# Another order for the first four chunks of a retention and FFN kernel, with block 0's squares on ScalarE

## The chip, the core and the metric

The kernel runs on one core of one Trainium2 chip. The metric is the time of one execution on the device in microseconds, as the median over several runs. Engines are named as the profile names them: PE is TensorE (PEld its weight loads), DVE is VectorE, ACT is ScalarE, POOL is GpSimd, SP is SyncE, which here only issues transfers.

## What is computed

Retention over 8 batches, 8 heads, 576 positions and a head size of 64, then a feed-forward layer over the 4608 tokens that come out of it:

```python
scores = scale * np.matmul(q, k.transpose(0, 1, 3, 2))
Dmat = np.where(rel >= 0, gamma[:, None, None] ** rel[None, :, :], 0.0)
attn = np.matmul(scores * Dmat, v)
x = attn.transpose(0, 2, 1, 3).reshape(4608, 512)
h = np.maximum(x @ w_in, 0.0)        # w_in: 512 x 2048
out = (h * h) @ w_out                # w_out: 2048 x 512
```

q, k and v are float32. The two weights are float64 and are brought to float32 inside the kernel.

## The kernel before, in words

**Tiling.** The tokens are cut into 36 chunks of 128 for the retention and into 9 blocks of 512 (four chunks each) for the feed-forward layer. The span has two parts: up to about 550 us the chunks are worked through and, between them, the first weight product of the blocks; after it comes the second product of all blocks. Both products use a scheme with seven multiplications in place of eight (`PRODUCTS`), except the first product of block 0, which is done plainly in 16 pieces (`first_in`, L698), one for each 128 columns of `w_in`.

**A chunk.** `load(i)` issues the transfers of q, k and v from SP (chunk 0's k and v from ACT). `scale_q` (L384) multiplies q by its decay, on POOL, for chunk 0 on DVE. `scale_v` (L488) does the same for v on POOL. `turn_in` (L435) transposes k and q on PE into PSUM, and `turn_out` (L444) copies the two halves back to SBUF, on ACT or DVE. For the first four chunks `scores_full` (L532) forms the 128 x 128 scores of each head, DVE masks them in two instructions (L536), `carry_full` (L551) adds what comes from earlier chunks, and `retain_full` forms the chunk's own part (L557) and the new state (L560). ACT then copies the result into `xT` (L572) and the state into `u_sb` (L494). Later chunks use `scores` (L470, masked at L481), `retain_a`, `retain_b` and `retain_c` (L514, L589, L595).

**A weight piece.** `fetch_raw` issues the transfer of a raw float64 piece of 512 KB (L205). `convert(n)` runs the next n of a piece's six parts: one and two on DVE (L219, L223), one called `beside` on ACT (L227, L228), then three more on DVE (L231, L234, L237). A `first_in(j)` needs piece j done to L237. It takes four matmuls, of 512 columns at most; with `halves` and `at` it does only a part of the block's 512 tokens: `(0,)` is the first 256, and `(0, C)` the first 128 of a half. ACT then writes the ReLU into `g_room` (L703), and the square, L706 on DVE, is put into a list, `queue`, from which `some(2)` takes up to two entries in each later `first_in`.

**Order.** The order of the work is written out by hand: each engine executes its instructions in the order in which the program issues them, and between engines semaphores wait. The first four chunks are a straight list of calls from `warm(5)` on; after it a loop goes over the chunks and calls `ffn`, which runs `convert(6)` and a `step()` (one `first_in`) once or twice per half chunk, until block 0 is done. `warm(n)` issues n matmuls on a constant tile whose result isn't used (L861). Transfers of SP are issued in program order; each waits for the one that is eight before it.

Of the kernel before, what the change touches and what calls it, by code (L numbers as in the profile page):

```python
# [15 lines left out]
C = 128  # L16
# [24 lines left out]
def kernel(  # L41
# [97 lines left out]
    def load(i, names="qkv"):  # L139
        if i == 0:  # L140
            nc.sync.dma_start(dv, decays)
        got = loaded.setdefault(i, [None] * 3)
        for name, pool, src in (("q", ld3, q), ("k", ld5, k), ("v", ld4, v)):
            if name not in names:
                continue
            t = got["qkv".index(name)] = pool.tile([128, H, D], F32, tag=name, name=f"{name}_ld")

            issue = nc.scalar if i == 0 and name != "q" else nc.sync
            b, c0 = divmod(i * C, S)
            runs = [(b, c0, slice(0, C))] if c0 + C <= S else [(b, c0, slice(0, CH)), (b + 1, 0, slice(CH, C))]  # L150
            for e in range(1 if name == "v" else 2):
                for b, c0, to in runs:
                    at = src[b, :, c0:c0 + to.stop - to.start, :].rearrange("h s d -> s h d")
                    if name == "v":
                        issue.dma_start(t[to], at)
                    else:
                        issue.dma_start(t[to, e * HP:(e + 1) * HP, :], at[:, e::2, :])
# [138 lines left out]
    def fetch_raw(count):  # L296

        for _ in range(count):
            if n_raw[0] < min(N_W1, n_made[0] + N_RAW):
                fetch_w(n_raw[0])  # L300
                n_raw[0] += 1
# [18 lines left out]
    def convert(count):  # L320
        for _ in range(count):
            f = next(w_in_steps, None)
            f and f()
# [7 lines left out]
    load(1, "qk")  # L331
    fetch_raw(1)
    load(1, "v")
    fetch_raw(1)
    load(2)
    fetch_raw(1)

    make_identity(nc, ident)

# [38 lines left out]
        clean.add((half, bank))  # L378
        return new

    def scale_q(i, engine):
        t = loaded[i][0]
        at = N_PAT + i % N_PAT
        engine.tensor_tensor(t, t, dv[:, :, at:at + 1].to_broadcast([C, H, D]), op=ALU.mult)  # L384

# [35 lines left out]
    def turn_in(i, js=(1, 0)):  # L423

        if "p" not in st[i]:
            if i < N_EARLY:
                p = [ps_e.tile([128, 512], F32, tag=f"e{h}", name="t_ps") for h in range(2)]
            else:
                t = ps_t[0].tile([128, 2, 512], F32, tag="t", name="t_ps")
                p = [t[:, h, :] for h in range(2)]  # L430
            st[i]["p"] = [x.rearrange("p (j d t) -> p j d t", j=2, d=HP) for x in p]
        for j in js:
            for hp in range(HP):
                for h in range(2):
                    nc.tensor.transpose(st[i]["p"][h][:, j, hp, :], loaded[i][j][rows(h), 2 * hp:2 * hp + 2, :],  # L435
                                        ident[rows(h), rows(h)])
# [48 lines left out]
    def scale_v(i):  # L485
        vs = st[i]["vs"] = loaded[i][2]
        at = i % N_PAT
        nc.gpsimd.tensor_tensor(vs, vs, dv[:, :, at:at + 1].to_broadcast([C, H, D]), op=ALU.mult)  # L488
# [37 lines left out]
    def scores_full(i):  # L526


        sc = st[i]["sc"] = [ps_f.tile([128, HP, C], F32, tag="f", name="sc_ps") for e in range(2)]
        for hp in range(HP):  # L530
            for e in range(2):
                nc.tensor.matmul(sc[e][:, hp, :], lhsT=st[i]["kT"][rows(e), hp, :], rhs=st[i]["qT"][rows(e), hp, :],  # L532
                                 start=True, stop=True, skip_group_check=True)
        r = st[i]["ret"] = ret_room[i % 2]
        for e in range(2):
            nc.vector.tensor_tensor(r[:, e, :, :], sc[e], msk_full.to_broadcast([C, HP, C]), op=ALU.mult)  # L536
        scale_v(i)

    def x_full(hp, e, b):
        return xp[0][rows(b), e, 0:256].rearrange("p (g t) -> p g t", g=2)[:, hp % 2, :]  # L540
# [1 line left out]
    def carry_full(i):  # L542

        xp[0] = ps_x.tile([128, 2, 256], F32, tag="x", name="x_ps", padded_shape=[128, 2, 512])
        clean.clear()
        if i == 0:
            u_ps[0] = ps_u.tile([128, HP, D], F32, tag="u", name="u_ps")
            return
        u = u_sb[2 * i % 3]
        for hp, e, b in HEADS[0:2] + HEADS[4:6] + HEADS[2:4] + HEADS[6:8]:  # L550
            nc.tensor.matmul(x_full(hp, e, b), lhsT=u[rows(e), hp, :], rhs=st[i]["qT"][rows(e), hp, :],  # L551
                             start=clears(b, e), stop=False, skip_group_check=True)

    def retain_full(i):

        for hp, e, b in (HEADS[j] for j in (0, 4, 2, 6, 1, 5, 3, 7)):
            nc.tensor.matmul(x_full(hp, e, b), lhsT=st[i]["vs"][:, head(hp, e), :], rhs=st[i]["ret"][:, e, hp, :],  # L557
                             start=clears(b, e), stop=False, skip_group_check=True)
        for hp, e, b in HEADS:
            nc.tensor.matmul(u_ps[0][rows(e), hp, :], lhsT=loaded[i][1][:, 2 * hp + e, :], rhs=st[i]["vs"][:, head(hp, e), :],  # L560
                             start=(i == 0 and hp == 0), stop=(hp == HP - 1), skip_group_check=True)
        x_out(i, lambda: grown(i, 1))
# [120 lines left out]
    def some(count=1):  # L683
        for f in queue[:count]:
            f and f()
        del queue[:count]

    def first_in(j, halves=(0, 1), at=(0, HT)):

        assert n_made[0] > j  # L690
        wi, m, e = pieces[j]
        mp, mm = divmod(m, 2)
        p = ps_f.tile([128, 2, HT], F32, tag="f", name="h_ps")
        w = w_in[mp][:, mm, 2 * e:2 * e + 2, :, :].rearrange("p s c f -> p (s c) f")
        lo, hi = halves[0], halves[-1] + 1
        p = p[:, lo:hi, at[0]:at[1]]
        for c in range(N_DM):
            nc.tensor.matmul(p, lhsT=w[:, c, :], rhs=xT[0][:, c, :].rearrange("p (h t) -> p h t", h=2)[:, lo:hi, at[0]:at[1]],  # L698
                             start=(c == 0), stop=(c == N_DM - 1))

        t = g_room[mp % 2][:, 2:5:2, mm, :] if e else g_room[mp % 2][:, 0:4:3, mm, :]
        t = t[:, lo:hi, at[0]:at[1]]
        nc.scalar.activation(t, p, AF.Relu)  # L703

        some(2)
        queue.append(lambda: nc.vector.tensor_tensor(t, t, t, op=ALU.mult))  # L706
        if mm and e and hi == 2 and at[1] == HT:
            queue.append(lambda: [nc.sync.dma_start(
                g_dram[0, a:b, :, 2 * mp:2 * mp + 2, :].rearrange("s p m t -> p s (m t)"),
                g_room[mp % 2][:, a:b, :, :].rearrange("p s m t -> p s (m t)")) for a, b in QUARTERS])  # L710
        if j >= N_W1 - 4:

            sums_w.setdefault(0, sum_w_in(0)).pop(0)()
            if n_next[0] > 1:
                if 1 not in sums_x:
                    sums_x[1] = sum_x(1)
                sums_x[1].pop(0)()
# [78 lines left out]

    def block_steps(n):
        if n == 0:
            seconds = [(0, first_in, j, (1,), (C, HT)) for j in range(N_HALF)]
            return seconds + [(0, first_in, j) for j in range(N_HALF, N_W1)]  # L800
        return [(n, ffn_in, n, mp, j) for mp in range(N_MP) for j in range(NP)]

# [55 lines left out]
    def warm(count):  # L858
        t = ps_f.tile([128, 512], F32, tag="f", name="idle_ps")
        for _ in range(count):  # L860
            nc.tensor.matmul(t[:, 0:256], lhsT=idle, rhs=idle[:, 0:1].to_broadcast([128, 256]), start=True, stop=True)  # L861
# [10 lines left out]
            load(i + 3, "v")  # L872

    warm(5)
    scale_q(0, nc.vector)
    turn_in(0, (1,))
    scale_q(1, nc.gpsimd)
    warm(1)
    turn_in(0, (0,))
    turn_out(0)  # L880
    load(3)
    fetch_raw(2)
    warm(1)
    scores_full(0)
    turn(1, (0, 0))
# [4 lines left out]
    scores_full(1)  # L890
    scale_q(2, nc.gpsimd)
    carry_full(1)
    convert(2)
    retain_full(1)
    load(4)
    fetch_raw(3)
    load(5)
    convert(3)
    first_in(0, (0,))
    convert(3)  # L900
    turn(2, (0, 0))
    scores_full(2)
    scale_q(3, nc.gpsimd)
    carry_full(2)
    first_in(1, (0,))
    convert(2)
    retain_full(2)
    load(6)
    turn(3)
    convert(1)  # L910
    scores_full(3)
    scale_q(4, nc.gpsimd)
    convert(3)
    carry_full(3)
    for j in range(N_HALF):
        first_in(j, (1,), (0, C))
    early.close()
    ps_t[0] = first.enter_context(tc.tile_pool(name="ps_t", bufs=1, space=PS))
    convert(2)
    retain_full(3)  # L920
    load(7)
    convert(1)
    step()
    step()
    convert(3)
# [2 lines left out]
    convert(3)  # L928
    scores(4)
    scale_q(5, nc.gpsimd)  # L930
    convert(3)
    step()
    convert(3)
    for i in range(N_EARLY + 1, N_CH + 1):
        if i > N_ONE:
            move(C, i)
# [289 lines left out]
```

## Time and profile before

| | |
|---|---|
| median of 3 runs | 957.81 us (957.13 to 959.32) |
| profiled execution, its time | 957.27 us |
| profiled execution, its span | 955.5 us |
| PE busy over the span | 939.5 us, 98% |
| DVE busy | 786.7 us, 82% |
| ACT busy | 335.7 us, 35% |
| POOL busy | 126.0 us, 13% |

The page cuts the span into 40 slices of 23.9 us. Its rows of busy tenths, the granted TensorE clock and the transfers are:

```profile
PE   8999999999999999999999999999999999999998
DVE  5789899888899898888856588788878788787876
ACT  3444485666765775766610000000000000000000
POOL 4312222212213212212100000000000000000000
PEclk9999999999999999999999999999999999999999
DMA  9996476775767765863369984535445453525251
```

A digit is the busy share of a slice in tenths. The first four to five slices hold all the work that this document is about: chunks 0 to 9 and the 16 pieces of block 0. The first slice is the one with the most idle PE; in it and the next two the 16 transfer engines are busy to nine tenths.

### The profile page before, as it was taken

What the parts mean: (1) busy time and instruction counts of PE and PEld (TensorE: products, weight loads), DVE (VectorE), ACT (ScalarE), POOL (GpSimd) and SP (SyncE); (2) the same over time, 40 slices, a digit from 0 to 9 for tenths busy, and PEclk for the clock granted to TensorE, in tenths of its full rate; (3) what the DMA queues carried; (4) which work ended last, traced back from release to release, by engine and by line L of the source; (5) the groups of instructions that cost most, each with busy time, mean ns of one, the idle gap of its engine ahead of it and who ended that gap; (6) DMA issues with size and microseconds to landing.
All of it is one profiled execution on the core that took longest, in us unless ns stands there. A gap on an engine that the chain in (4) does not pass through costs nothing. (4 is left out here: it accounts for less than half of the span.)

```text
span 955.5 us, 23378 instructions
## 1 busy us (share of the span) xinstructions
PE 939.5 (98%) x9750; PEld 844.1 (88%) x9750; DVE 786.7 (82%) x1435; ACT 335.7 (35%) x798; POOL 126.0 (13%) x115
## 2 busy tenths in 40 slices
PE   8999999999999999999999999999999999999998
PEld 6654788888888888888888899999999999999998
DVE  5789899888899898888856588788878788787876
ACT  3444485666765775766610000000000000000000
POOL 4312222212213212212100000000000000000000
PEclk9999999999999999999999999999999999999999
DMA  9996476775767765863369984535445453525251
GB/s 228 235 278 147 131 222 159 208 234 181 199 182 237 216 183 172 274 187 117 144 212 353 354 282 168 187 114 186 170 154 190 172 190 142 199 100 176 93 174 45
DMA packets 172778, 181.43 MB, mean 190 GB/s; under 512 B 118784, under 2 KB 133248, under 8 KB 166016
## 3 DMA queue, kind: packets, MB, share of 16 engines
q1 hardware_dynamic: 170576, 179.41, 60.2%
q8 instruction: 76, 1.25, 0.6%
q10 hardware_dynamic: 2096, 0.52, 0.3%
q14 instruction: 30, 0.25, 0.1%
HBM read 109.39 MB, written 70.52 MB: 188 GB/s over the span
## 5 line engine op out<-in xcount | busy, mean ns | idle before, releaser
L734 PE MATMUL h_b<-room,w 128*128 128x256 f32 x768 | 182.0, 380 | 2.3 <-DVE room L753 1.9
L420 ACT COPY qk<-flip 32x256 f32<-32x256 f32 x416 | 167.4, 402 | 6.6
L734 PEld LDWEIGHTS h_b<-room,w 128*128 128x128 f32 x768 | 145.4, 190 | 23.5 <-DVE room L753 3.2
L1075 PE MATMUL o_b<-w,room 128*128 128x128 f32 x1168 | 144.4, 275 | 0.2 <-DVE room L1027 0.2
L1075 PEld LDWEIGHTS o_b<-w,room 128*128 128x128 f32 x1168 | 137.2, 192 | 0.4 <-DVE room L1027 0.4
L734 PE MATMUL h_a<-room,w 128*128 128x256 f32 x512 | 124.0, 384 | 0.8 <-issue 0.7
L1075 PE MATMUL o_c<-w,room 128*128 128x128 f32 x1008 | 123.0, 275 | 0.0
L734 PE MATMUL h_c<-room,w 128*128 128x256 f32 x512 | 121.0, 379 | 0.0
L1075 PEld LDWEIGHTS o_c<-w,room 128*128 128x128 f32 x1008 | 117.7, 192 | 0.0
L1089 ACT COPY r<-o_a 128x128 f32<-128x128 f32 x53 | 14.1, 266 | 271.9 <-PE o_a L1075 236.2
L734 PEld LDWEIGHTS h_c<-room,w 128*128 128x128 f32 x512 | 97.3, 190 | 13.2
L734 PEld LDWEIGHTS h_a<-room,w 128*128 128x128 f32 x512 | 95.1, 190 | 14.8 <-issue 1.2
L1075 PE MATMUL o_a<-w,a 128*128 128x128 f32 x688 | 85.6, 275 | 0.0
L751 POOL TENSOR_TENSOR room<-room 128x512 f32<-128x512 f32 x32 | 35.1, 1096 | 360.1 <-ACT room L750 284.4
L1075 PEld LDWEIGHTS o_a<-w,a 128*128 128x128 f32 x688 | 81.2, 192 | 0.1
L741 DVE SCALAR_TENSOR_TENSOR room<-room 128x512 f32<-128x512 f32 x96 | 73.5, 765 | 3.3
L698 PE MATMUL h_ps<-room,w 128*128 128x512 f32 (+2 forms) x160 | 59.6, 518 | 4.0 <-DVE w L237 2.6
L488 POOL TENSOR_TENSOR v_ld<-v_ld,dv 128x512 f32<-128x512 f32 x36 | 51.4, 1429 | 8.9 <-DMA v_ld<-in_v_dram 6.0
L753 DVE TENSOR_TENSOR room<-h_b,room 128x512 f32<-128x512 f32 x32 | 22.0, 688 | 37.0 <-PE h_b L734 37.0
L698 PEld LDWEIGHTS h_ps<-room,w 128*128 128x128 f32 x160 | 26.8, 190 | 28.1 <-issue 20.7
L595 PEld LDWEIGHTS x_ps<-qk,v_ld 64*64 64x64 f32 x1024 | 38.4, 134 | 12.7 <-issue 10.9
L595 PE MATMUL x_ps<-qk,v_ld 64*64 64x64 f32 x1024 | 48.3, 222 | 0.0
(113 smaller groups left out, 1352.1 us busy)
## 6 DMA issues: line engine op xcount, KB each, us to landing
g_dram<-room SPq DMA_DIRECT2D x164, 256.0 KB, 3.9
a<-g_dram SPq DMA_DIRECT2D x30, 1024.0 KB, 5.9
room<-g_dram SPq DMA_DIRECT2D x15, 1024.0 KB, 6.1
w<-w_dram SPq DMA_DIRECT2D x7, 1792.0 KB, 10.7
out_dram<-room SPq DMA_DIRECT2D x17, 512.0 KB, 3.3
q_ld<-in_q_dram SPq DMA_DIRECT2D x64, 128.0 KB, 4.3
w<-in_moe_w_in_dram SPq DMA_DIRECT2D x16, 512.0 KB, 6.3
w<-in_moe_w_out_dram SPq DMA_DIRECT2D x16, 512.0 KB, 4.4
```

Source lines behind the costliest of these rows:

```text
L420: nc.scalar.copy(*moves.pop(0)[2:])
L488: nc.gpsimd.tensor_tensor(vs, vs, dv[:, :, at:at + 1].to_broadcast([C, H, D]), op=ALU.mult)
L595: return [lambda hp=hp, e=e, b=b: nc.tensor.matmul(x_at(hp, e, b, h), lhsT=s["vs"][rows(h), head(hp, e), :], rhs=s["ret"][rows(h), e, hp, ...
L698: nc.tensor.matmul(p, lhsT=w[:, c, :], rhs=xT[0][:, c, :].rearrange("p (h t) -> p h t", h=2)[:, lo:hi, at[0]:at[1]], start=(c == 0), stop= ...
L734: nc.tensor.matmul(p[:, mm, :], lhsT=w[:, c, :], rhs=xs[n][right][:, c, :], start=(j in OPENS and mm == 0 and c == 0), stop=(j in CLOSES a ...
L741: nc.vector.scalar_tensor_tensor(t, t, 0.0, t, op0=ALU.max, op1=ALU.mult)
L751: nc.gpsimd.tensor_tensor(g["A11"], g["A11"], g["A11"], op=ALU.mult)
L753: nc.vector.tensor_tensor(g["A22"], p, p15, op=ALU.add)
L1075: nc.tensor.matmul(p, lhsT=s["lefts"][left][:, m, :], rhs=w_out[j][:, m, WO_SLOT[right], :], start=(i in OPENS and m == 0), stop=(i in CLO ...
L1089: nc.scalar.copy(r[:, 0, 0:128], p)
```

## The change

It has five parts.

1. Loads: chunk 2's q and k are issued ahead of the second raw weight piece, and its v behind it. The third raw piece is no longer issued between chunk 2 and chunk 3, but behind chunk 3 (`fetch_raw(3)` in place of `fetch_raw(2)`).
2. Chunk 0: its q is scaled in two halves of four heads; its v is scaled on POOL ahead of chunk 1's q, where it stood behind it; one of the single `warm` matmuls is gone.
3. Chunks 1 to 3: `turn(2)` stands right behind `retain_full(1)`, and `turn(3)` between `carry_full(2)` and `retain_full(2)`, each earlier by one `first_in`. Pieces 0 and 1 run over the first half of the block in two parts of 128 tokens each, placed behind a turned chunk or in front of a retain, and over the second half in one part of 256, where the second half was in two parts.
4. Conversion: the parts are put elsewhere between the chunks, in groups of three, and the last two groups ahead of the loop hold six parts each, so that 36 parts (six pieces) are issued ahead of the loop in place of 33.
5. Squares: where a `first_in` covers both halves (pieces 2 to 15), the square is an ACT instruction (`Square`) and no longer one of DVE; `some(2)` now stands ahead of the piece's own ReLU.

```diff
     load(1, "v")
+    load(2, "qk")
     fetch_raw(1)
-    load(2)
-    fetch_raw(1)
+    load(2, "v")
...
-    def scale_q(i, engine):
-        t = loaded[i][0]
+    def scale_q(i, engine, parts=(slice(0, H),)):
         at = N_PAT + i % N_PAT
-        engine.tensor_tensor(t, t, dv[:, :, at:at + 1].to_broadcast([C, H, D]), op=ALU.mult)
+        for heads in parts:
+            t = loaded[i][0][:, heads, :]
+            engine.tensor_tensor(t, t, dv[:, heads, at:at + 1].to_broadcast(list(t.shape)), op=ALU.mult)
...
-        scale_v(i)
+        if i:
+            scale_v(i)
...
+        some(2)
         nc.scalar.activation(t, p, AF.Relu)
-
-        some(2)
-        queue.append(lambda: nc.vector.tensor_tensor(t, t, t, op=ALU.mult))
+        if hi - lo == 2:
+            queue.append(lambda: nc.scalar.activation(t, t, AF.Square))
+        else:
+            queue.append(lambda: nc.vector.tensor_tensor(t, t, t, op=ALU.mult))
...
-            seconds = [(0, first_in, j, (1,), (C, HT)) for j in range(N_HALF)]
+            seconds = [(0, first_in, j, (1,)) for j in range(N_HALF)]
...
-    scale_q(0, nc.vector)
+    scale_q(0, nc.vector, (slice(0, HP), slice(HP, H)))
     turn_in(0, (1,))
+    scale_v(0)
     scale_q(1, nc.gpsimd)
-    warm(1)
     turn_in(0, (0,))
     turn_out(0)
     load(3)
-    fetch_raw(2)
+    fetch_raw(3)
...
     carry_full(1)
+    retain_full(1)
     convert(2)
-    retain_full(1)
+    turn(2, (0, 0))
     load(4)
     fetch_raw(3)
     load(5)
+    first_in(0, (0,), (0, C))
     convert(3)
-    first_in(0, (0,))
-    convert(3)
-    turn(2, (0, 0))
+    first_in(0, (0,), (C, HT))
     scores_full(2)
     scale_q(3, nc.gpsimd)
     carry_full(2)
-    first_in(1, (0,))
-    convert(2)
+    turn(3)
     retain_full(2)
     load(6)
-    turn(3)
-    convert(1)
+    convert(3)
     scores_full(3)
     scale_q(4, nc.gpsimd)
-    convert(3)
     carry_full(3)
-    for j in range(N_HALF):
-        first_in(j, (1,), (0, C))
+    first_in(1, (0,), (0, C))
     early.close()
...
-    convert(2)
+    convert(3)
     retain_full(3)
+    first_in(1, (0,), (C, HT))
+    convert(3)
     load(7)
-    convert(1)
     step()
     step()
...
-    convert(3)
+    convert(6)
     step()
-    convert(3)
+    convert(6)
```

## The prediction

> **What bounds the kernel now.** I read the whole span first: PE is busy for 939.5 of 955.5 us, so there are 16 us of idle PE in all, and only what shortens them, or PE's own work, can shorten the time. The chain of waits, followed back from the end, runs over PE's second product and tells nothing of the start. So next come the stages that the change touches, as busy time of the engines in three stretches. The columns are the stretch, its length, busy PE, PEld, DVE, ACT and POOL (instructions in brackets), the granted clock, the share of transfers and GB/s.
>
> ```profile
> 0.00:35.00 35.00, 29.15 (x382) 24.12 (x382) 21.43 (x35) 14.70 (x29) 12.14 (x21) 1.00 1.00 232
> 35.00:70.00 35.00, 34.85 (x403) 17.90 (x400) 29.59 (x48) 17.06 (x32) 8.20 (x7) 1.00 0.95 259
> 70.00:104.00 34.00, 31.37 (x437) 16.45 (x436) 32.37 (x49) 13.51 (x27) 7.81 (x6) 1.00 0.52 126
> ```
>
> PE idles 5.85 us up to 35 us, none to speak of up to 70, and 2.63 us from 70 to 104, where DVE is busy for 95% and ACT for 40%. Two separate prizes, then. The lists of waits say what PE waited for (us in total, times, longest); the last line is of 70 to 100 us, the others of 0 to 35.
>
> ```profile
> PE sc_ps L532 <- DVE qk L444: 1.2, 2, 0.9
> PE sc_ps L532 <- ACT qk L444: 1.2, 1, 1.2
> PE idle_ps L861 <- DVE w L329: 1.1, 1, 1.1
> PE h_ps L698 <- ACT w L227: 1.0, 1, 1.0
> PE x_ps L557 <- POOL v_ld L488: 0.5, 1, 0.5
> PE t_ps L435 <- DVE q_ld L384: 0.4, 1, 0.4
> ...
> PE h_ps L698 <- DVE w L237: 2.6, 3, 1.2
> ```
>
> Up to 35 us PE mostly stands between a turn and its scores, while the turned chunk is copied; in block 0 it waits three times for a converted weight. After 104 us PE is the bound again, so a shift at 104 us reaches the end. The rows that the sums use, in order of time (start, duration):
>
> ```profile
> 14.76 1.06 POOL L384 TENSOR_TENSOR q_ld<-q_ld,dv 128x512 f32<-128x512 f32 x1 [1.48 <-DMA q_ld<-in_q_dram]
> 14.93 1.43 DVE L237 SCALAR_TENSOR_TENSOR w<-w,w 128x512 uint32<-128x512 uint32 x1
> 18.17 1.38 POOL L488 TENSOR_TENSOR v_ld<-v_ld,dv 128x512 f32<-128x512 f32 x1 [2.35 <-DMA v_ld<-in_v_dram]
> 20.28 1.16 PE L532 MATMUL sc_ps<-qk 64*128 64x128 f32 x16 [1.16 <-ACT qk L444]
> 21.03 1.06 POOL L384 TENSOR_TENSOR q_ld<-q_ld,dv 128x512 f32<-128x512 f32 x1 [1.48 <-DMA q_ld<-in_q_dram]
> 39.34 3.70 PE L698 MATMUL h_ps<-room,w 128*128 128x512 f32 x8
> 98.10 3.70 PE L698 MATMUL h_ps<-room,w 128*128 128x512 f32 x8 [1.17 <-DVE w L237]
> ```
>
> And the groups of 35 to 104 us (busy, mean ns | idle before, releaser):
>
> ```profile
> L706 DVE TENSOR_TENSOR room<-room 128x512 f32<-128x512 f32 x13 | 8.9, 683 | 0.0
> L228 ACT ACTIVATE w<-w,exp_bias 128x512 uint32<-128x512 uint32 x12 | 8.7, 721 | 25.0 <-DVE w L219 25.0
> L227 ACT ACTIVATE w<-w 128x512 f32<-128x512 uint32 x12 | 8.3, 688 | 0.0
> ```
>
> **Chunk 0.** q's scaling is one instruction of 0.69 us at 6.05; two halves of 0.42 (the 128x256 squares, 416 ns) let the first four transposes start before the second half is done, so q's turn ends some 0.3 us earlier. Against it, v0 lands at 7.64 (issued 1.84, 5.8 to landing) and holds POOL to 8.70; chunk 1's q, scaled 8.20 to 9.26 now, then runs to 9.76 and its turn ends near 10.25 (now 9.8). The product that waited for v0 until 10.33 now finds it, and starts behind that turn at 10.25. Net: 0.1 us gained, which I count as nothing; ends -0.4 and +0.5.
>
> The warm matmul that goes (0.70 us from 5.66) stood in idle time. [...] Here the gap becomes 0.4 to 0.8 us, and the profile grants 1.00 even with gaps of 1.2. By the row: 0. [...] I take 0.
>
> **Chunks 1 to 3.** Transfers run at 232 GB/s here, about 1.1 us for 256 KB and 2.1 for a raw piece. Chunk 2's q, now scaled at 14.76, leaves piece 1 behind itself and lands near 12.8; POOL is with v1 until 13.27, so it is scaled by 14.35 (now 15.82). v2 has the same bytes ahead of it as before: 18.17. Chunk 3's q loses piece 2 ahead of it: near 19 (now 21.03), but POOL holds v2 until 19.55, so it is ready at 20.6. PE then, with durations of its rows:
> - chunk 1 ends at 15.5 as now; turn(2) to 16.2; meanwhile piece 0 is done on DVE at 15.7, not 16.36, since its last step no longer meets POOL's scaling (1.43 us where the clear ones take 0.69);
> - two parts of piece 0, 1.02 each, to 18.25. ACT's two copies of the turned chunk (1.07) run beside them, which is the 1.2 us wait of today. Scores(2) start at 18.25 (now 20.28) and end at 19.4, carry(2) at 20.0;
> - turn(3): k, then q at 20.65, to 21.05: a wait of 0.6, which is new, with retain(2) behind it. The mask (19.5 to 20.8) is ready, so retain(2) takes 21.05 to 22.55, beside chunk 3's copies on ACT and DVE (to 21.8); scores(3) to 23.7 (now start 27.01);
> - piece 1 on DVE behind that copy: three steps, one against v3's scaling on POOL, done at 24.3, and the mask of chunk 3 behind them to 25.6. Carry(3) to 24.3, a part of piece 1 to 25.35, retain(3) to 26.85, the other part to 27.8;
> - the second halves of pieces 0 and 1, 1.96 each, to 31.7. ACT has `xT` of chunk 3 at 27.6, just in time. turn(4), whose q lands at 28.36 as now, to 32.4 (now 35.1); piece 2 to 36.0, scores(4) to 36.6.
>
> Then **a new wait**: piece 3 needs L237, and on DVE its last three steps stand behind chunk 4's copy, which waits for ACT's copy, which stands behind ACT's ReLU (31.7 to 32.1), L227 and L228 (to 33.4). DVE copies until 34.7, squares a half (0.4), and takes 2.1 more: 37.1. Piece 3 starts at 37.2, 0.6 late. Now it starts at 39.34. **Gain of the head: 2.1 us.** Its low end is 0, if chunk 3's q still comes at 21.03 (every step from turn(3) on is then some 2 us later); its high end 3.2, if the new waits vanish.
>
> **Squares and conversion from 37 us on.** DVE loses 14 squares, 0.60 us apart back to back, or 8.4 us; ACT gains 14. [...] The square stands ahead of the next ReLU and behind L227 and L228; its own ReLU ended a piece (3.4 us) ago, so it stalls nothing. The instruction list of the changed kernel has one activation table load, as now.
>
> Against PE: piece 11 is ready at 77.21 today; eight squares fewer (4.8) and 0.8 for the later piece 3 give 73.2, and PE wants it at 77.27 - 0.57 - 2.1 = 74.6. Piece 14: 86.1 against 88.4. Piece 15: at most 91.6 against 93.4. Slack everywhere, about one or two collisions with POOL (0.75 each), so **2.6 us gained** (ends 1.2 and 2.6). The half piece of extra lead in the conversion costs no instruction and adds to that slack. The last square falls where ACT idles 1.5 and 3.9 us (104 to 111): nothing.
>
> **Sum.** Head 2.1 + block 0 2.6 = 4.7 us. The profiled execution took 957.27, so 952.6; the median of the runs lies 0.54 above it, so 957.81 - 4.7 = **953.1 us**. Behind 104 us one PE wait of 1.5 (at 145, for DVE with POOL beside it) may come or go; I leave it and widen by it.
>
> **Rivals.**
> - *The transfers don't follow the new order* (15 in 100): the three streams share the same engines, v2 and chunk 3's q land as now, and the head gains 0. For: the share of transfers is 1.00 up to 35 us. Against: landings today follow bytes issued. 957.8 - 2.6 = 955.2.
> - *One wait replaces another in block 0* (10 in 100): L231 waits for L227/L228, which stand behind squares; PE still waits for L237. 957.8 - 2.1 = 955.7. [...]
> - *ACT paces block 0* (slower, 7 in 100): each square holds ACT, and behind it the ReLU that frees PSUM, then the conversion. [...]
> - *More than the sum* (6 in 100): the wait at 145 goes too: 951.6.
>
> The forecast itself has the rest, 62 in 100. Within 0.2% (1.9 us, about what this kernel's runs can tell from no change) fall the low ends of the first two rivals, 12 in 100 in all; slower is the third rival and 1 more. Faster 0.80, same 0.12, slower 0.08. The range goes from 950.8 (head 3.2, block 0 2.6, the wait at 145 partly) to 956.5 (head 0, block 0 1.3).
>
> **What would show it.** Scores(2) at 18.3, scores(3) at 22.6, piece 2 at 32.4 and piece 3 at 37.2; chunk 3's q scaled from 19.6; no PE wait for L237 from 70 to 104, DVE there near 80% busy and ACT near 60%. It is wrong if chunk 3's q comes at 21, if piece 3 starts near 39, or if PE waits for a weight with ACT's L228 late.

## The result, and the profile after

The changed kernel takes 953.00 us (median of 4 runs, 952.74 to 954.21) beside 958.57 us for the kernel before on the same chip (4 runs, 957.13 to 960.01). The ratio is 0.9944 with a 95% interval of 0.9926 to 0.9963, so some 5.4 us are gone. The forecast was 953.1.

The profiled execution of the changed kernel took 954.21 us (span 952.5) and is the slowest of its four, where the one before, 957.27, was among the fastest of its kernel. So the two profiles differ by only 3.0 us in the span. A second profile of the unchanged new kernel (after_again, below) has a span of 950.5, which is 5.0 less. The shift is therefore followed place by place, with both profiles.

First the busy time of the engines of the changed kernel in the same three stretches as before:

```profile
0.00:35.00 35.00, 31.93 (x386) 25.65 (x387) 19.63 (x37) 14.89 (x30) 12.13 (x21) 1.00 0.95 216
35.00:70.00 35.00, 34.40 (x419) 17.51 (x421) 30.57 (x48) 21.61 (x40) 9.12 (x7) 1.00 1.09 282
70.00:104.00 34.00, 34.00 (x449) 20.31 (x442) 27.59 (x41) 18.56 (x35) 8.11 (x6) 1.00 0.52 133
```

PE is busy for 2.8 us more of the first 35 us, and from 70 to 104 it doesn't idle at all. DVE there fell from 95% to 27.59 / 34 = 81%, and ACT rose from 40% to 55%. The list of what PE waited for (us in total, times, longest) has five lines from 0 to 35 us; the last two are of 35 to 70, and from 70 to 104 there is none:

```profile
PE idle_ps L865 <- DVE w L329: 1.1, 1, 1.1
PE x_ps L553 <- ACT u_sb L495: 0.6, 1, 0.6
PE h_ps L700 <- DVE w L237: 0.4, 1, 0.4
PE sc_ps L533 <- DVE qk L445: 0.3, 1, 0.3
PE t_ps L436 <- DVE q_ld L385: 0.2, 1, 0.2
...
PE h_ps L700 <- DVE w L237: 0.3, 1, 0.3
PE sc_ps L471 <- DVE qk L445: 0.3, 1, 0.3
```

The three waits of scores for a turned chunk's copies up to 35 us (2.4 us in all before) are down to one of 0.3, and the wait of the first piece for ACT (1.0) and the three of 70 to 104 us (2.6) are gone. The rows of the changed kernel in order of time (start, duration), for the instructions that the prediction dated. The view of piece 3 ends at 40 us, so it counts seven of its eight matmuls:

```profile
18.37 1.16 PE L533 MATMUL sc_ps<-qk 64*128 64x128 f32 x16
19.65 1.06 POOL L385 TENSOR_TENSOR q_ld<-q_ld,dv 128x512 f32<-128x512 f32 x1
22.64 1.16 PE L533 MATMUL sc_ps<-qk 64*128 64x128 f32 x16
24.83 1.16 PE L700 MATMUL h_ps<-room,w 128*128 128x128 f32 x8 [0.42 <-DVE w L237]
32.59 3.70 PE L700 MATMUL h_ps<-room,w 128*128 128x512 f32 x8
37.23 3.27 PE L700 MATMUL h_ps<-room,w 128*128 128x512 f32 x7 [0.32 <-DVE w L237]
98.70 1.99 PE L738 MATMUL h_a<-room,w 128*128 128x256 f32 x8
```

The kernel before begins block 1 here:

```profile
103.75 1.99 PE L734 MATMUL h_a<-room,w 128*128 128x256 f32 x8
```

Scores(2) start at 18.37 where they started at 20.28, scores(3) at 22.64 (27.01), piece 3 at 37.23 (39.34), and block 1 at 98.70 (103.75). And the groups of the changed kernel from 35 to 104 us (busy, mean ns | idle before, releaser):

```profile
L708 ACT ACTIVATE room<-room 128x512 f32<-128x512 f32 x14 | 8.7, 620 | 0.0
L228 ACT ACTIVATE w<-w,exp_bias 128x512 uint32<-128x512 uint32 x12 | 8.7, 721 | 8.4 <-DVE w L219 8.3
```

L708 is the new square: 0.620 us each, and it never waited. ACT's idle time for DVE ahead of L228 fell from 25.0 to 8.3 us: its slack was spent and not exceeded.

**Where the gain goes afterwards.** The same product of PE, found in two traces, tells how far one runs ahead of the other. Below is the lead over the trace before, in us:

| place (time before) | after | second profile of after |
|---|---|---|
| block 1 begins (103.75) | 5.05 | 5.32 |
| about 153 | 5.04 | 5.34 |
| about 327 | 6.00 | 6.26 |
| about 370 | 2.37 | 4.36 |
| end of the first product (537) | 2.67 | 4.65 |
| end of the span | 3.01 | 5.00 |

The lead at 104 us is a little over the forecast 4.7 in these two traces; in a third with the same instructions up to there (e7_w_out_later, below) it is 3.40. Between 327 and 370 us some of it is lost, 3.6 us in one trace and 1.9 in the other. What PE waited for from 104 to 560 us in the changed kernel:

```profile
PE h_b L738 <- DVE room L757: 1.9, 2, 1.5
PE h_a L738 <- issue: 1.7, 1, 1.7
PE sc_ps L471 <- ACT qk L421: 0.5, 1, 0.5
PE h_b L738 <- DVE room L750: 0.3, 1, 0.3
```

The second line is new in its size. "issue" means that the engine stood still without waiting for anything that the profile shows. It is this row of the timeline:

```profile
333.62 0.69 PE L738 MATMUL h_a<-room,w 128*128 128x256 f32 x1 [1.67 <-issue]
```

Right behind it the granted clock (the number behind the last bracket) is at half for one stretch, and full again in the next:

```profile
333.70:337.20 3.50, 3.50 (x9) 2.79 (x10) 3.50 (x7) 0.30 (x1) 0.00 (x0) 0.51 0.64 168
337.20:340.70 3.50, 3.50 (x18) 3.09 (x17) 1.04 (x3) 3.37 (x9) 0.00 (x0) 1.00 0.94 258
```

PE gets through nine matmuls where the next stretch has eighteen. The half clock lasts 3.41 us, so by this trace it costs about 1.7 us on top of the stop of 1.67; together they are nearly all of the 3.6.

### The profile page after: what moved, and what is told of

The parts are those of the page before. It is cut to its first block, busy times and chain, and to the rows that moved or that the text cites. A ratio compares the mean times of both kernels' runs of the same rounds, so it can differ in the third digit from the quotient of the medians.

```text
span 952.5 us, 23368 instructions
## 1 busy us (share of the span) xinstructions
PE 940.9 (99%) x9748; PEld 845.9 (89%) x9748; DVE 777.9 (82%) x1422; ACT 344.0 (36%) x812; POOL 126.9 (13%) x115
## 5 line engine op out<-in xcount | busy, mean ns | idle before, releaser
L757 DVE TENSOR_TENSOR room<-h_b,room 128x512 f32<-128x512 f32 x32 | 22.0, 689 | 37.6 <-PE h_b L738 37.6
```

The costliest lines, as they stand in the source:

```text
L757: nc.vector.tensor_tensor(g["A22"], p, p15, op=ALU.add)
```

## The experiments

Four questions: is the head's gain one of the transfers or of the order of the products; do the squares or the larger lead of the conversion free PE in block 0; what does chunk 0's part do; and where do the 1.9 to 3.6 us go behind 327 us. Each kernel is timed beside the kernel before on the same chip, and the ratio compares those two. The chips differ a little: the kernel before had medians of 958.78 beside e1 to e4, 959.23 beside e5 to e7 and after_again, and 958.13 beside e8 to e11. "Piece 3" and "block 1" are their starts in the kernel's profile; e5 and e6 were timed once only.

| kernel | median us (runs) | ratio (95%) | piece 3 | block 1 |
|---|---|---|---|---|
| before | 958.57 (4) | | 39.34 | 103.75 |
| after | 953.00 (4) | 0.9944 (0.9926 to 0.9963) | 37.23 | 98.70 |
| e1_dve_squares | 954.73 (10) | 0.9968 (0.9956 to 0.9981) | 37.33 | 100.61 |
| e2_act_squares_alone | 954.51 (8) | 0.9961 (0.9947 to 0.9975) | 39.01 | 100.59 |
| e3_old_loads | 955.02 (8) | 0.9970 (0.9957 to 0.9982) | 39.22 | 101.33 |
| e4_new_loads_alone | 958.71 (8) | 1.0007 (0.9994 to 1.0021) | 39.68 | 105.99 |
| e5_old_chunk0 | 951.84 (1) | | 37.87 | 99.33 |
| e6_less_lead | 952.32 (1) | | 37.58 | 98.53 |
| after_again | 952.66 (2) | 0.9929 (0.9909 to 0.9949) | 36.86 | 98.43 |
| e7_w_out_later | 950.67 (4) | 0.9907 (0.9891 to 0.9924) | 37.93 | 100.35 |
| e8_lead_alone | 955.77 (6) | 0.9972 (0.9960 to 0.9984) | 39.76 | 103.33 |
| e9_dve_squares_less_lead | 956.11 (5) | 0.9997 (0.9961 to 1.0033) | 37.16 | 100.55 |
| e10_one_more_warm | 951.83 (4) | 0.9929 (0.9912 to 0.9945) | 37.55 | 99.58 |
| e11_warm_w_out | 951.22 (4) | 0.9925 (0.9910 to 0.9940) | 36.94 | 98.98 |

One thing to keep in mind for every row: three of these traces (after, after_again, e7_w_out_later) execute the very same instructions up to block 1, and their piece 3 starts at 37.23, 36.86 and 37.93, their block 1 between 98.43 and 100.35. A difference of under 1 us between two single traces of the head, or of under 2 at block 1, is weak evidence by itself; where two times bear on the same question, both are given. Taken together, the traces are firmer. The nine kernels or repeats with the new loads and the new order start piece 3 at 36.86 to 37.93 (middle value 37.33), the five that lack one or both at 39.01 to 39.76 (39.34). From piece 3 to block 1, the nine with the squares on ACT need 60.95 to 62.42 us (61.58), the five with them on DVE 63.28 to 66.31 (63.57). In neither case do the two groups overlap, and each step is worth 2.0 us by the middle values.

### The head: order of loads, order of products

The changed kernel with the loads in the old order:

```diff
-    load(2, "qk")
     fetch_raw(1)
-    load(2, "v")
+    load(2)
+    fetch_raw(1)
...
-    fetch_raw(3)
+    fetch_raw(2)
```

> The changed kernel with the loads in the order of before. Theory (the turned chunks can only move up because their q lands earlier): chunk 3's q is scaled at 21.0, turn(3) ends near 22.5, piece 3 starts at 38.5 to 39.3, so the head loses 1.3 to 2 of its 2.1 us; block 1 near 100.5. Rival (the order of the products does it, loads are early enough anyway): piece 3 within 0.4 us of 37.2.

Piece 3 started at 39.22: the new order of the products without the new loads gains nothing up to there. PE's list of waits from 0 to 36 us has a line that the first profiles of the two kernels lack (after_again has it with 0.3), and the timeline shows chunk 3's q scaled 1.9 us later than in the changed kernel:

```profile
PE t_ps L436 <- DMA k_ld<-in_k_dram: 1.2, 3, 0.8
```

```profile
21.57 1.06 POOL L385 TENSOR_TENSOR q_ld<-q_ld,dv 128x512 f32<-128x512 f32 x1 [1.72 <-PE sc_ps L533]
```

The row names PE's scores as what released POOL, but the second half of this q landed at 21.41, just before it (in the changed kernel at 19.49), so the transfer alone would have held it nearly as long. PE now waits for the transfer of a chunk's k, and turns chunk 2 at 17.20 (15.74 in the changed kernel) and chunk 3 at 22.1 (20.2). The kernel before with the new loads alone, the same edit the other way round:

> The kernel before with the new order of loads and nothing else changed. Theory: PE's order holds the turns behind the first pieces, so little is gained; piece 3 at 38.7 to 39.5, block 1 at 103.0 to 104.0. Rival (transfers alone are the bound of the head): piece 3 at 37.2 to 38.

The head gains nothing (39.68, just outside the expected 38.7 to 39.5), and the time is that of the kernel before. Block 1 at 105.99 was not expected; the trace puts it on one line (36 to 104 us):

```profile
PE h_ps L698 <- DVE w L237: 4.6, 4, 2.0
```

Five steps of DVE between 41 and 52 us fell on POOL's scalings and took 1.27 to 1.55 us each where the clear ones take 0.42 to 0.69. The median of its eight runs (958.71) shows no loss against the kernel before (958.78). This profile (959.21) is near that median, while the one of the kernel before that it is set against (957.27) lies below the median of its own; whether the collisions are of this execution alone was not tried. What follows: each half alone brings nothing up to piece 3, and the two together bring 2.1 us. The first turns need both the early q and k and an early place in the order. (That order was changed together with the splitting of pieces 0 and 1 and the places of the conversion parts; these were not tried apart.)

### Block 0: squares or lead

The changed kernel with the squares back on DVE:

```diff
         t = t[:, lo:hi, at[0]:at[1]]
-        some(2)
         nc.scalar.activation(t, p, AF.Relu)
-        if hi - lo == 2:
-            queue.append(lambda: nc.scalar.activation(t, t, AF.Square))
-        else:
-            queue.append(lambda: nc.vector.tensor_tensor(t, t, t, op=ALU.mult))
+
+        some(2)
+        queue.append(lambda: nc.vector.tensor_tensor(t, t, t, op=ALU.mult))
```

> The changed kernel with all squares of block 0 back on DVE; everything else is kept. Theory (head and block 0 are two separate gains): piece 3 starts at 37.2 as in the changed kernel, 2.1 earlier than before; PE waits again for L237 from 65 to 104 us, 2 to 3 us in all; block 1's first matmul starts near 101.7 (changed kernel 98.7, before 103.75), so some 2 us faster than before. Rival (the half piece of lead in the conversion did it, not the move to ACT): block 1 starts at 98.7 to 99.5 and the waits for L237 stay away.

And the kernel before with this edit of the change alone, the same lines the other way round:

> The kernel before with block 0's squares on ACT and nothing else changed. Theory: head as before (piece 3 at 39.3), no PE wait for L237 from 70 to 104, block 1 at 103.75 - 2.6 to 2.9 = 100.9 to 101.2. Rival (a wait for ACT takes the place of the wait for DVE without the extra lead): PE still waits 1 us or more for a weight, block 1 after 102.3.

The second did what it should. Its busy times from 35 to 104 us show DVE at 79% and 83% and a PE without a gap from 70 on:

```profile
35.00:70.00 35.00, 34.51 (x397) 17.71 (x397) 27.74 (x45) 20.42 (x38) 9.17 (x7) 1.00 0.98 267
70.00:104.00 34.00, 34.00 (x452) 19.28 (x451) 28.25 (x42) 18.73 (x36) 7.53 (x6) 1.00 0.52 131
```

From piece 3 to block 1 it needs 2.83 us less than the kernel before, and its time is lower by 0.39% (3.7 us). The first (e1_dve_squares) bears out neither theory: block 1 at 100.61 lies between the two forecasts, and the waits for L237 that were to come back did not. The same view of it shows:

```profile
35.00:70.00 35.00, 33.61 (x395) 17.30 (x394) 33.10 (x54) 18.24 (x32) 6.93 (x6) 1.00 1.00 268
70.00:104.00 34.00, 33.48 (x450) 19.19 (x449) 32.71 (x46) 14.05 (x27) 10.19 (x8) 1.00 0.55 141
```

DVE is busy for 95% and 96%, so it is full. PE's waits from 36 to 104 us are here 0.9 for the transfer of a k, 0.5 for DVE's copy of a turned chunk and 0.3 for L237. A theory from that: the larger lead of the conversion only moves the wait to other work of DVE. The next two kernels test it: the kernel before with three more parts converted ahead of the loop, and the changed kernel with the squares on DVE and three parts fewer.

```diff
     convert(3)
     step()
-    convert(3)
+    convert(6)
```

> The kernel before with half a piece more of conversion ahead of the loop (36 parts in place of 33) and nothing else changed; squares on DVE. Theory (either the lead or the move of the squares is enough to end the waits for L237 at the end of block 0, since the conversion comes to lead by a half piece or falls back by eight squares): the 2.6 us of such waits from 70 to 104 us shrink to under 1 us, block 1 starts at 101 to 102.5. Rival (only the move of the squares ends them, and the run with the squares back on DVE lacked them because other waits had put PE late): 2 us or more of waits stay, block 1 at 103 or later.

```diff
-    convert(6)
+    convert(3)
     step()
     convert(6)
```

(The second diff stands on top of that of e1_dve_squares.)

> The changed kernel with the squares on DVE and without the extra half piece of lead, so with neither of the two things that could end the waits for L237. Theory: 2 us or more of waits for L237 from 50 to 104 us come back, block 1 starts at 101.3 to 102.5. Rival (neither matters once the head is in its new order): no such waits, block 1 as with the lead, 100.6 or earlier.

PE's waits from 36 to 104 us, first with the lead alone, then with neither squares on ACT nor lead:

```profile
PE x_ps L595 <- DVE qk L481: 1.2, 1, 1.2
PE sc_ps L470 <- DVE qk L444: 0.7, 1, 0.7
```

```profile
PE h_ps L700 <- DVE w L237: 2.1, 4, 1.2
```

With the lead, PE waits for DVE's mask (L481) and DVE's copy of a turned chunk; without it, for the weight. The sum is about the same, 1.9 and 2.1 us. That much fits, and so does block 1 of the second: 100.55, as early as with the lead (100.61 in e1_dve_squares), where its theory had it at 101.3 or later. The times don't settle it: block 1 of the first starts at 103.33, only 0.4 us before that of the kernel before, while its six runs are 0.28% faster (2.7 us), of which the profiled one is the slowest (956.67); and the second's runs scatter from 953.35 to 964.8, so its time says nothing. How much the lead is worth on a DVE that is full stays open. Last, the changed kernel with squares on ACT but without that lead:

```diff
-    convert(6)
+    convert(3)
     step()
     convert(6)
```

> The changed kernel with three conversion parts ahead of the loop's last step in place of six, so that the conversion leads by half a piece less, as before. Theory: DVE has slack once the squares are gone; block 1 within 0.3 us of 98.7. Rival (the lead is what removes the waits for L237): 1 us or more of such waits come back, block 1 at 99.7 or later.

Block 1 at 98.53 against 98.70 and 98.43: as soon as DVE has room, the lead is not needed. So the squares carry block 0's gain: 2.83 us on the kernel before, and inside the changed one some 1.9 us (100.61 against 98.70), which is within the scatter of single traces. The groups of nine and five traces above back it, and so do the times: the ratio of e1_dve_squares, 0.9968, lies above both of the changed kernel, 0.9944 and 0.9929, though its interval overlaps the first one's.

### Chunk 0

The changed kernel with chunk 0 as it was:

```diff
-        if i:
-            scale_v(i)
+        scale_v(i)
...
-    scale_q(0, nc.vector, (slice(0, HP), slice(HP, H)))
+    scale_q(0, nc.vector)
     turn_in(0, (1,))
-    scale_v(0)
     scale_q(1, nc.gpsimd)
+    warm(1)
```

> The changed kernel with chunk 0 as before: q scaled in one instruction, v behind chunk 1's q on POOL, the warm matmul back. Theory: the split of q gains what v's new place on POOL costs, so chunk 1's scores and all that follows start within 0.2 us of the changed kernel; piece 3 at 37.0 to 37.4, granted clock 1.00 in both. Rival (the chunk 0 edits carry part of the head's gain): piece 3 0.4 us or more later.

Piece 3 came at 37.87, 0.64 later than in the first profile of the changed kernel, as the rival had it, but within the scatter of that same program (36.86 to 37.93). The part is worth less than can be seen in one trace: this does not contradict the forecast's "nothing", and a few tenths either way cannot be told.

### What is lost behind 327 us

A second profile of the unchanged new kernel:

> The changed kernel once more, unchanged, for its trace. In its profiled execution PE stood 1.7 us with no recorded reason at 332 us, and the granted clock was half for the 3.4 us after that, together 3.6 us. Theory (a chance event of that execution): block 1 starts at 98.7 again, the stop is elsewhere or absent, and the span is 949 to 951.5. Rival (the changed kernel causes it): again a stop of over 1 us near 332 us with half clock behind it, span 952.5.

The half clock did not come again, but the stop did: 1.63 us at 333.3. So the stop is no chance event of one execution. The half clock behind it comes and goes: of six traces with this stop, two have it (after and e1_dve_squares). Runs without a profile have their mean granted clock on record too, and one such stretch lowers it to 0.998. It is 0.998 or less in 9 of 30 runs of the kernels whose trace has the long stop, and in 4 of 85 runs of the others. In e1, e3 and e4 these runs are 1.7 to 2.3 us slower in the mean than the rest of their kernel's. So the half clock is rare without the stop and not certain with it.

Across all traces there is a pattern. PE stops at the same instruction of its list (4045 recorded matmuls stand ahead of it), for 1.4 to 1.7 us, in six of the seven traces of kernels that have one warm matmul fewer than before (after, after_again, e1, e3, e6, e9; e7 has only a stop of 0.3 near 405). It does so in none of the seven traces of kernels with as many PE instructions as before (before, e2, e4, e5, e8, e10, e11). Six of those seven stop elsewhere, near 220, for 0.45 to 0.69. The seventh, e11, stops near 404 for 0.53. A theory from that: the place where the stop falls, and its length, hang on how many instructions PE's list has ahead of it. It was tested by giving back one warm matmul, where PE is idle:

```diff
-    warm(5)
+    warm(6)
```

> The changed kernel with warm(6) in place of warm(5): PE has as many instructions ahead of everything later as before the change, whose warm matmul stood elsewhere. Five of six traces of kernels without that matmul show PE stopping for 1.6 to 1.7 us at the same instruction of its list (start 331 to 336 us), none of the four traces with it does; those stop 0.65 us at another one near 220 us. Theory (the stop belongs to the place in PE's instruction stream, with what the transfers do just then): no stop over 1 us near 332, 0.6 us near 218, the span about 1 us shorter than the changed kernel's, 949.5. Rival (the stop is caused by something else in the changed kernel): it stays at 1.6 us.

Of PE's waits from 104 to 560 us in this kernel, the one without a recorded reason is now:

```profile
PE h_a L738 <- issue: 0.4, 1, 0.4
```

The stop of 1.7 is gone, and one of 0.4 stands at 218 us, where the kernel before has its 0.69. Its lead over the trace before goes from 4.17 at block 1 to 5.13 at the end, where that of the second profile of after goes from 5.32 to 5.00. (Each lead begins with what its own head scattered by.) That is 0.96 gained against 0.32 lost, so the missing matmul costs 1.3 us in these traces. e5_old_chunk0, which has the matmul back in its old place, agrees: 4.42 to 5.40, and a stop of 0.65 at 218. The times do not show it: the ratio, 0.9929, is that of after_again. The theory holds in part. The count of PE's instructions moves the stop, but it does not decide alone: e7_w_out_later has the very PE list of the changed kernel and stops only for 0.3 near 405.

What goes with the stop shows in the transfers of after between 329 and 334 us (packets, MB, share of the 16 engines' time):

```profile
q8 instruction: 1, 0.02, 1.2%
```

One packet of instructions (16 KB) started at about 331.2 and took 0.92 us, and the stop ended at 333.62. In all fourteen traces each such stop of the block products (16 in all, near 220, 333 and 405) ends 2.2 to 2.5 us behind the start of such a packet (331.03 and 333.31 in after_again, 333.76 and 336.17 in e3, 220.22 and 222.66 before), while in e10 and e7, which don't stop near 333, the same packet starts at 327.1 and 328.3. This queue has 76 packets in the execution of after, and PE has one or two such stops in a trace, of up to 1.7 us each. That PE stands still because such a packet comes late is argued from the times and not shown by an experiment, and why the packet starts late in one kernel and in time in the other was not found.

### The wait near 145 us

In the changed kernel, where this wait falls at 140 us, DVE takes two long steps of a conversion (L231, L234) ahead of L757, which PE's product needs:

```profile
136.59 1.53 DVE L231 SCALAR_TENSOR_TENSOR w<-w,w 128x512 f32<-128x512 uint32 x1
138.16 1.43 DVE L234 TENSOR_TENSOR w<-w,w 128x512 f32<-128x512 f32 x1
139.51 0.68 DVE L757 TENSOR_TENSOR room<-h_b,room 128x512 f32<-128x512 f32 x1
```

With one part of `w_out` not issued there, so that a later place takes it:

```diff
-        for _ in range(0 if busy[0] else 2 if late_w2 > 1.5 and j in (0, 3) else late_w2 > 0):
+        for _ in range(0 if busy[0] or (n, mp, j) == (1, 2, 3) else 2 if late_w2 > 1.5 and j in (0, 3) else late_w2 > 0):
```

> The changed kernel with one more edit: in block 1, third pair of columns, fourth product, no part of w_out's conversion is issued; it catches up in later steps. It aims at the PE wait of 1.5 us near 140 us, for DVE's L757 behind two conversion steps that POOL slows. Theory: that wait is gone, block 2 and the end come 1.0 to 1.5 us earlier than in the changed kernel. Rival (the step that is put off makes another wait a few products later): the lead at the end of the first product is within 0.4 us of the changed kernel's.

In its timeline the two steps no longer stand ahead of L757, which now waits for PE and not the other way round:

```profile
138.72 0.69 DVE L757 TENSOR_TENSOR room<-h_b,room 128x512 f32<-128x512 f32 x1 [0.39 <-PE h_b L738]
```

Its lead over the trace before grows by 1.6 us there (from 3.40 to 5.01). Half of that goes back near 458 us (from 5.55 to 4.79), where the same two steps (L231 at 455.31, L234 at 456.82) now stand ahead of L757. PE's wait there is 1.1 us instead of 0.5, and it is the only one for L757 that is listed from 104 to 560 us:

```profile
PE h_b L738 <- DVE room L757: 1.1, 1, 1.1
```

The rest of what this trace gains on after_again is not of this wait: the stop of 1.63 near 333 is absent. At the end of the first product its lead is 4.79, within 0.4 of after_again's 4.65, as the rival had it. Both edits together:

> The changed kernel with both edits: w_out's conversion put off in that one step, and warm(6). Theory: the two gains add where both apply, span 948.5 to 950, so the fastest of all kernels here. Rival (the run with the put-off step owed its time to the missing stop alone): no faster than either edit alone.

The lead of its trace is 6.52 us behind the wait near 145, 7.43 at about 327, 5.81 at the end of the first product and 6.15 at the end: the largest of all traces. But most of what it gains near 145 (from 4.77 to 6.52) goes back between 334 and 500 us (from 7.43 to 5.81), so that from block 1 to the end it gains 1.38 where e10_one_more_warm gains 0.96. With the stop already gone, the put-off step is worth 0.4 us in these traces.

In the times, all four runs of e7_w_out_later (950.40 to 952.07) lie below the two of after_again on the same chip (952.25 and 953.07), by about 2 us in the median; the intervals of the ratios, 0.9907 and 0.9929, overlap. e11_warm_w_out (951.22) and e10_one_more_warm (951.83), on another chip, cannot be told apart, and the ratio of e11, 0.9925, is nearly that of after_again. So that the put-off step gains is likely and small; that the two edits add up is not shown.

## Why the prediction was right

**Head, 2.1 us: right, by its own steps.** Scores(2) were forecast at 18.3 and came at 18.37; chunk 3's q from 19.6, 19.65; scores(3) at 22.6, 22.64; piece 2 at 32.4, 32.59; piece 3 at 37.2 and 0.6 late, 37.23 and 0.32 late. The gain to piece 3 is 39.34 - 37.23 = 2.11. Four of these five agree within 0.1 us, closer than two traces of the same program agree, so part of that is luck; by the middle values of nine and five traces the gain is 2.0. Two inputs were off without harm: 512 KB at 232 GB/s takes 2.3 us and not 2.1, and chunk 2's q was scaled at 13.86, some 0.6 later than in the working, because POOL had v1 until 13.89; PE turned the chunk only at 15.74. Two small waits were not foreseen: carry(1) stands 0.6 us for ACT's state copy (L495), which is behind ACT's two parts of piece 0, and piece 1 stands 0.42 us for L237. Piece 2 was 0.2 us late behind them, and piece 3, which waits for DVE, no longer. That the transfers would follow the new order, the uncertain step, was right (chunk 3's q landed at 19.49 against near 19); e3 and e4 show that the step was needed.

**Chunk 0, nothing: not contradicted.** e5 lies in the scatter, so a few tenths either way stay open.

**The warm matmul, 0 us: the one term that was mis-sized.** The prediction weighed it by the idle time around it and by the clock, and the clock there indeed stayed at 1.00 (4 to 8 us, before and after). What it missed is that the matmul is also an entry in PE's list: without it, a stop without a recorded reason falls at about 333 us with 1.4 to 1.7 us and no longer at 220 with 0.45 to 0.69. By the traces of e10 and after_again that costs 1.3 us. The half clock behind it came after a gap of 1.67 us, lasted 3.41 us and cost about 1.7 us of that trace. The sum hides it, for the gain by the ratios is larger than forecast all the same (below). The lead at 104 us was 5.05, 5.32 and 3.40 in three traces, where 4.7 stood.

**Block 0, 2.6 us: right in kind and nearly in size.** From piece 3 to block 1 the changed kernel gained 5.05 - 2.11 = 2.94 us on the one trace before; by the middle values of the nine and five traces it is 2.0, inside the 1.2 to 2.6 that the prediction gave. The waits for L237 between 70 and 104 us went, DVE is at 81% (80 forecast), ACT at 55% (60). The square costs 0.620 us on ACT, less than the 0.683 of DVE's square before and than the 0.688 and 0.721 of L227 and L228, ACT's nearest rows before. ACT had the room for it: it was busy for 30.57 of the 69 us from 35 to 104 before, and is for 40.17 now. e8 narrows the reason: with the squares on DVE and more lead, PE waits for DVE's mask and copy in place of the weight. So it is DVE's load as a whole that held PE, and the wait for the weight was only where it showed. The prediction had the larger lead adding slack, at no price; with the squares moved it adds nothing that can be seen (e6).

**The wait near 145, left out: it stayed,** with 1.5 us (140.2 in the changed kernel).

**The sum.** The forecast set the gain of 4.7 against the profiled execution and moved it to the median of the shown runs. The kernel before gave medians of 958.13 to 959.23 in the four comparisons, so the 957.81 it started from was a little low, and the gain, 5.4 to 6.8 us by the ratios of after and after_again, a little larger than 4.7. That 953.1 met 953.00 to 0.1 us is in part luck: the four runs scatter by 1.5 us, the start was 0.8 us below the median beside the changed kernel (958.57), and the stop cost 1.3 us that no term held. What made up for both is not shown place by place, because the profile before, with 957.27, itself lies 1.3 us below that median.

**The rivals.** "The transfers don't follow" fell with chunk 3's q at 19.65. "One wait replaces another in block 0" did not happen in the changed kernel; something like it is what e8 shows with the squares on DVE, though there the new waits are for DVE's mask and copy. "ACT paces block 0" fell with ACT at 55% and a square that waits for nothing. "More than the sum" needed the wait near 145 to go, and it stayed; e7 shows that it can be removed, but that about half of it comes back near 458 us.

## What to carry to other kernels

When one engine is full and the wait list names one of its instructions, an earlier start for that instruction may only hand the wait to the next one (in e8 to DVE's mask and copy, 1.2 and 0.7 us); move work to an engine with idle time, and price it by that engine's own rows (here 0.620 us a square, on an ACT busy for 44% before). A new order of products and a new order of loads may each be worth nothing alone (here piece 3 at 39.22 and 39.68, and at 37.23 with both): date the landing and the use of every chunk, and change both. After an edit that gains early in the span, follow the lead from place to place to the end: here even an idle matmul taken away moved a stop of PE from 220 to 333 us, and a wait removed at 140 us came back in part at 458.

## What was not expected of the hardware

- PE stopped at a fixed place of its instruction list near 333 us, for 1.4 to 1.7 us in six of seven traces, and for 0.4 us at another place with one matmul more ahead of it. Each such stop ended 2.2 to 2.5 us behind the start of an instruction packet.
- The granted clock fell to half for 3.41 us behind a gap of only 1.67 us in the changed kernel, and for as long behind one of 1.73 in e1; behind gaps of 1.4 to 1.7 at the same place in four other traces it did not. What decides it was not tried. Over all runs, a mean clock of 0.998 or less is more frequent in the kernels with this gap (9 of 30) than in the others (4 of 85).
- Piece 3 starts up to 1.1 us apart in three executions (36.86 to 37.93), although no instruction up to there differs.
